# Interleaving runs of 8 words instead of halves 256 words apart in the moving operands of the dense products

## The chip, the core and the metric

The program runs on one core of a Trainium2 chip: TensorE (PE) multiplies, ScalarE (ACT), VectorE (DVE) and GpSimd (POOL) work on vectors, SyncE (SP) issues the transfers. The metric is the device time of one execution in microseconds (us), lower is better. A product on PE has a stationary operand, loaded first, and a moving operand, of which it takes one column after the other from the on-chip memory (SBUF); its sums go to PSUM.

## What is computed

Attention over 4 x 8 heads of 576 positions, a soft mixture of 8 experts, and then a dense part, which the change is about:

```python
def _moe2_ref(x, w_in, w_out):            # x 2304 x 512, w_in 512 x 2048, w_out 2048 x 512
    h = x @ w_in
    g = np.where(h > 0.0, h, np.exp(np.minimum(h, 0.0)) - 1.0)
    return (g @ w_out).astype(np.float32)
```

`w_in` and `w_out` arrive as 64-bit floats and are made 32-bit ones on the chip.

## The kernel before

The mixture's result has rank 32, so its output is never formed. `c4` holds the combining weights of the tokens and `M4` the 32 expert slots times `w_in`, and `h` is the product of the two. Both are kept as a high and a low part, stacked over the 128 partitions. `emit_ct` copies parts of `c4` into `cTf` (the first 2304 words of the tile `pers`): for each of the 4 stacked blocks `a` and each batch `b` of 576 tokens, cut where a group of 512 tokens ends, by ACT, POOL or DVE.

The dense part is a list of units. A unit is a group of 512 tokens (the last group has 256) and one of 16 slices `f` of 128 hidden columns. For each there is one product `hps` (`f_h`, L1276) of 128 x 512, then on ACT and DVE the function (`f_e` L1282, `f_r` L1285, `f_g` L1288) and a high and a low part of the result (L1294, L1298), then for each 128 tokens three products of 128 x 512 into one PSUM tile (`f_o`, L1329 to L1331: high x high, high x low, low x high), in the format fp32r. The very first unit (256 tokens) does it in full 32-bit format with one product, which runs as two passes (L1322). At the end of a run of units a sum is taken out of PSUM (L1364 on ACT, L1366 and L1370 on DVE).

Beside this run the decodes of the weights, per 128 x 512 words: one instruction on ACT that reads every second word (`dec_abs`, L992), and three on DVE (L996, and L1000 and L1006, which read every second word of the 64-bit tile), and for `w_out` a high and a low part (L1225, L1228). `w_in` goes on through `m_nodes` (L1165 to L1192) into `M4`; the products L1183 and L1184 there are the only fp32r ones of 128 x 512 whose moving operand is read word after word.

The order of the dense part is made by a planner (`list_order`): each step is a node with an assumed cost, what it needs and a due time, and the steps are written out engine by engine in the planner's order. The cost that `decode_nodes` gives to `dec_abs` is one of these numbers.

The two helpers `turns` and `pairs` say in which order an operand's columns are walked. In the kernel before, `turns` takes the first word of the first half, the first word of the second half, the second word of the first half and so on, so that consecutive words are 256 words (1 KB) apart in a 512-word slice. What lies in the operand is permuted to fit: the host permutes the columns of `w_out`, and `emit_ct` writes `cTf` in that order. The results come out in natural order, and `pairs` on an output is the same as walking it word after word.

Of the kernel before, what the change touches and what calls it, by code (L numbers as in the profile page):

```python
# [9 lines left out]
F32R = mybir.dt.float32r  # L10
I32 = mybir.dt.int32
BF16 = mybir.dt.bfloat16
AF = mybir.ActivationFunctionType
# [6 lines left out]
def attn_moe_mlp(ctx, tc, q, k, v_l, v_s, phi, w1, w2, w_in, w_out, out):  # L20
    nc = tc.nc
    B, S, D = 4, q.shape[2] // 4, 64
    NT, DM = out.shape
# [44 lines left out]
        39: (-7.7, 3.0), 232: (-14.4, 9.2), 964: (0.0, 14.7),  # L68
    }
    FULL = 1  # L70
    PO, PH = 0.648, 0.216
    FT, FW, M0 = 7.5, 0.9, ((0, 128), (128, 128), (256, 256))

    const = ctx.enter_context(tc.tile_pool(name="const", bufs=1))
# [168 lines left out]
    for x in ORDER:  # L243
        p = {"L": 0, "S": 2}[x]
        p += cnt_p[p] == (6 if p == 0 else 4)
        c = cnt_p[p]
# [10 lines left out]
    with tc.manual_schedule():  # L257
# [18 lines left out]
        for b in range(B):  # L276
            lm = lcur[32 * b:32 * b + 32]
            nc.gpsimd.affine_select(
                out=lm, in_=lm, compare_op=ALU.is_ge, fill=0.0, base=0, pattern=[[-1, 32]], channel_multiplier=1,
# [4 lines left out]
            out=lkeep[:, 0], in0=lkeep[:, 1], scalar1=0.0, scalar2=None, op0=ALU.is_equal  # L284
# [8 lines left out]
        for b in range(B):  # L293
# [3 lines left out]
                out=sm_, in_=sm_, compare_op=ALU.is_ge, fill=0.0, base=0, pattern=[[-1, MR]], channel_multiplier=1,  # L297
# [140 lines left out]
        for n, (p, t, h) in enumerate(units):  # L438
# [4 lines left out]
            else:  # L443
                c = 1152 * t + 576 * h
# [579 lines left out]
        M4 = pers[:, NT:NT + DFF].bitcast(F32R)  # L1024
        e0r = e0.bitcast(F32R)

        groups = [(t, min(512, NT - t)) for t in range(0, NT, 512)]

        def turns(v):
            return v.rearrange("p (a x) -> p x a", a=2)  # L1030

        def pairs(v):
            return v.rearrange("p (x a) -> p x a", a=2)

        def emit_ct(eng, a, b):
            for t0, n in groups:
                u0, u1 = max(t0, S * b), min(t0 + n, S * b + S)
                if u0 >= u1:
                    continue
                o = turns(cTf[32 * a:32 * a + 32, t0:t0 + n])[:, (u0 - t0) // 2:(u1 - t0) // 2]  # L1040
                i = pairs(c4[32 * b:32 * b + 32, a // 2, u0 - S * b:u1 - S * b].bitcast(F32R))
                if eng == "A":
                    nc.scalar.activation(out=o, in_=i, func=AF.Copy)
                else:
                    (nc.vector if eng == "V" else nc.gpsimd).tensor_copy(out=o, in_=i)

        for e in range(NE - 1):
            emit_w2(e)
# [49 lines left out]
        ps_out = ctx.enter_context(tc.tile_pool(name="ps_out", bufs=6, space=PSUM))  # L1098

        NF = DFF // 128  # L1100
        dec_of = {("w", 0, c): dec[:, c] for c in range(4)}
        wo_hi, wo_lo = {}, {}
        wo_hi[0], wo_lo[0] = slot(2, "wh0"), slot(4, "wl0")
# [14 lines left out]
        def node(eng, dur, deps, key, fn, alloc=None, at=0.0):  # L1118
            kd, hold = HOLD.get(len(nodes), (0.0, -9.0))
            nodes.append((eng, dur, list(deps), key + kd, fn, alloc, max(at, hold)))  # L1120
            return len(nodes) - 1
# [16 lines left out]
        def decode_nodes(kind, i, c, key, rel, h0=0):  # L1138
            at = loads.get((1 - kind, i, c), loads.get((1 - kind, i), 0.0))
            deps = [] if at else [dma[1 - kind, i]]  # L1140
            k, z, h = ("ow"[kind], i, c), (512 - h0) / 512, slice(h0, 512)

            def f_abs():
                if not h0:
                    cnt["dec"] += 1
                    dec_of[k] = dec[:, cnt["dec"] % 8]
                dec_abs(w64[1 - kind, i][:, c, h], dec_of[k][:, h])

            def step(f):
                return lambda: f(w64[1 - kind, i][:, c, h], dec_of[k][:, h])  # L1150

            n = node("A", 0.05 + 0.47 * z, deps, key - 3.0, f_abs, None if h0 else ("dec", rel), at)
            n = node("V", 0.065 + 0.27 * z, [n], key - 2.0, step(dec_1))
            n = node("V", 0.07 + 0.53 * z, [n], key - 1.4, step(dec_2))
            n = node("V", 0.07 + 0.53 * z, [n], key - 0.7, step(dec_3))
            d3[1 - kind, i, c, h0] = n
            return n
# [57 lines left out]
        def w_tile(d, s, f):  # L1215
            if f // 8 not in d:
                d[f // 8] = slot(s, f"w{f}")
            return d[f // 8][:, 512 * (f % 8):512 * (f % 8) + 512]
# [49 lines left out]
        def unit_nodes(u):  # L1268
            si, gi, f, f0, f1 = work[u]
            t0, n = groups[gi]  # L1270
            z, T, t = n / 512, due[u], {}
            rel_h, rel_g, rel_hi, rel_lo = [], [], [], []

            def f_h():
                t["ps"] = ps_h.tile([128, 512], F32, tag="h", name="hps")[:, 0:n]
                nc.tensor.matmul(  # L1276
                    pairs(t["ps"]), M4[:, 128 * f:128 * f + 128], turns(cTf[:, t0:t0 + n]), start=True, stop=True
                )

            def f_e():  # L1280
                t["g"] = p2.tile([128, 512], F32, tag="g", name="g", bufs=3)[:, 0:n]
                nc.scalar.activation(out=t["g"], in_=t["ps"], func=AF.Exp)  # L1282

            def f_r():
                nc.scalar.activation(out=t["g"], in_=t["g"], func=AF.Relu, scale=-1.0, bias=1.0)  # L1285

            def f_g():
                nc.vector.scalar_tensor_tensor(  # L1288
                    out=t["g"], in0=t["ps"], scalar=0.0, in1=t["g"], op0=ALU.max, op1=ALU.subtract
                )  # L1290

            def f_hi():
                t["hi"] = ring("hi")[:, 0:n]
                nc.scalar.activation(out=t["hi"], in_=t["g"], func=AF.Copy)  # L1294

            def f_lo():
                t["lo"] = ring("lo")[:, 0:n]
                nc.vector.tensor_tensor(out=t["lo"], in0=t["g"], in1=t["hi"].bitcast(F32), op=ALU.subtract)  # L1298

            def link(k, x):  # L1300
                if k in chain:
                    nodes[x][2].append(chain[k])
                chain[k] = x
                return x

            x = link("h", node("P", PH * z, [m_done[f]], T - 4.1 - SL, f_h, ("h", rel_h)))
            x = link("e", node("A", 0.05 + 0.43 * z, [x], T - 3.7 - SL, f_e, ("g", rel_g)))
            x = node("A", 0.09 + 0.43 * z, [x], T - 3.0 - SL, f_r)
            x = node("V", 0.07 + 0.53 * z, [x], T - 2.3 - SL, f_g)
            rel_h.append(x)  # L1310
            full = u < FULL
            if not full:
                x = link("hi", node("A", 0.09 + 0.43 * z, [x], T - 1.5 - SL, f_hi, ("hi", rel_hi)))
                x = link("lo", node("V", 0.07 + 0.53 * z, [x], T - 0.8 - SL, f_lo, ("lo", rel_lo)))
                rel_g.append(x)
            for s in range(n // 128):
                def f_o(s=s):
                    if f == f0:
                        ops[si, gi, s] = ps_out.tile([128, DM], F32, tag="o", name="ops")
                    o, c = ops[si, gi, s], slice(128 * s, 128 * s + 128)  # L1320
                    if full:
                        nc.tensor.matmul(  # L1322
                            pairs(o), t["g"][:, c], turns(dec_of["o", f // 4, f % 4]), start=(f == f0), stop=False
                        )
                        return
                    hi, lo = turns(w_tile(wo_hi, 0, f).bitcast(F32R)), turns(w_tile(wo_lo, 5, f).bitcast(F32R))
                    for x in halves(u, s):
                        y, q = pairs(o[:, x]), slice(x.start // 2, x.stop // 2)
                        nc.tensor.matmul(y, t["hi"][:, c], hi[:, q], start=(f == f0), stop=False)  # L1329
                        nc.tensor.matmul(y, t["hi"][:, c], lo[:, q], start=False, stop=False)  # L1330
                        nc.tensor.matmul(y, t["lo"][:, c], hi[:, q], start=False, stop=(f == f1 - 1 and x.stop == 512))  # L1331

                rel_o = []
                y = link("o", node("P", 0.9 if full else PO, [x, d3[1, f // 4, f % 4, 0] if full else w_done[f]],
                                   T + PO * s, f_o, ("o", rel_o) if f == f0 else None))
                if full:
                    rel_g.append(y)
                    w_rel[f].append(y)
                else:
                    rel_hi.append(y)  # L1340
                    rel_lo.append(y)
                if f == f0:
                    o_rel.append(rel_o)
                    o_due.append(T + PO * s)
                    part_n[si, gi, s] = len(o_rel) - 1
                if f == f1 - 1:
                    ev_n.append((si, gi, s, f0, f1, y, T + PO * s, halves(u, s)))
# [51 lines left out]
def _lay(np, q, k, v, moe_phi, **rest):  # L1399
# [15 lines left out]
    w1, w2 = ((w.reshape(w.shape[0], -1, 128, w.shape[2]).transpose(0, 2, 1, 3).reshape(w.shape[0], 128, -1))  # L1415
              for w in (rest["moe_w1"], rest["moe_w2"]))
    wo = rest["moe2_w_out"]
    wo = wo.reshape(wo.shape[0], -1, 2).transpose(0, 2, 1).reshape(wo.shape)
    return dict(rest, moe2_w_out=wo, q=lay(q), k=lay(k), v_l=vl, v_s=vs, moe_phi=phi, moe_w1=w1, moe_w2=w2)


# [23 lines left out]
```

## Time and profile before

| | us |
|---|---|
| median of 3 runs (353.8 to 354.85) | 354.21 |
| the profiled execution | 354.27 |
| its span, first to last instruction | 352.6 |
| busy in the span: PE, DVE, ACT, POOL | 332.7, 268.7, 256.3, 63.1 |

The dense part starts at 128 us of the span and ends with it. Before it lie attention (to about 84 us) and the experts, of which the last weights land at 124 us. [...] A product's recorded duration, 379 ns for 128 x 512, overlaps the next one's; the distance between two starts is what a product costs. The same holds for ACT and DVE when they have no gap: there the distance from start to start counts.

### The profile page before, as it was taken

Reading aid. Unit: us, or ns where it says so; the run is one execution under the profiler, and the core shown is the slowest. Engines: PE = TensorE matmul, PEld = TensorE weight load, DVE = VectorE, ACT = ScalarE, POOL = GpSimd, SP = SyncE. Lnnn points to the kernel's source line nnn. Section 1 sums busy time; section 2 is a strip of 40 time slices with the busy share of each in tenths; the row PEclk is TensorE's granted clock in tenths of the full one; section 3 lists DMA queues with packets and bytes.
Section 4 is the critical chain, followed back from the end, with each engine's and each line's share of the span. In section 5 each row is a group of like instructions: output and inputs, shape, how many; then the busy total and the mean of one; then the engine's idle time right before and its main releaser. Section 6 shows DMA issues by size and latency. Waiting matters only on the chain.

```text
span 352.6 us, 7011 instructions
## 1 busy us (share of the span) xinstructions
PE 332.7 (94%) x2679; PEld 251.4 (71%) x2679; DVE 268.7 (76%) x576; ACT 256.3 (73%) x494; POOL 63.1 (18%) x114
## 2 busy tenths in 40 slices
PE   5789889999999999999999999999999999999995
PEld 4678776773233356687887588887878888888884
DVE  6899888744705349999999999999984775576752
ACT  9588999983217359999998786966676666666660
POOL 8888534530209200000000000000000000000000
PEclk9999999999999999999999999999999999999999
DMA  7999999999999999670000606000000011033301
GB/s 270 403 414 414 424 416 422 425 412 421 420 432 416 407 400 374 231 269 0 3 0 0 241 0 237 3 0 0 2 0 2 2 59 59 2 119 119 119 3 60
DMA packets 15329, 70.51 MB, mean 200 GB/s; under 512 B 1600, under 2 KB 2112, under 8 KB 12352
## 3 DMA queue, kind: packets, MB, share of 16 engines
q1 hardware_dynamic: 15296, 70.06, 49.8%
q8 instruction: 21, 0.34, 0.4%
q14 instruction: 12, 0.10, 0.1%
HBM read 65.34 MB, written 4.72 MB: 199 GB/s over the span
## 4 chain that ended last, share of the span: by engine, by line
PE 55%; DVE 17%; ACT 15%; DMA 8%; issue 3%; POOL 2%; DVEq 0%; SPq 0%; POOLq 0%; ACTq 0%
PE ops L1329 13%; PE ops L1331 13%; PE ops L1330 13%; DMA q<-in_moe_w_dram 6%; PE hps L1276 3%; PE s_ps L924 3%; ACT xw L992 2%; ACT bd L658 2%; ACT g L1285 2%; DVE sc L590 2%; ACT g L1282 2%; PE o_ps L671 2%; ACT part L1364 2%; DVE g L1288 2%; DVE xw L1006 2%
## 5 line engine op out<-in xcount | busy, mean ns | idle before, releaser
L1288 DVE SCALAR_TENSOR_TENSOR g<-hps,g 128x512 f32<-128x512 f32 (+1 forms) x80 | 51.1, 639 | 13.1 <-ACT g L1285 12.7
L1282 ACT ACTIVATE g<-hps 128x512 f32<-128x512 f32 (+1 forms) x80 | 45.3, 567 | 8.7 <-PE hps L1276 7.5
L1285 ACT ACTIVATE g<-g 128x512 f32<-128x512 f32 (+1 forms) x80 | 47.9, 599 | 1.3
L1294 ACT ACTIVATE ghi<-g 128x512 fp32r<-128x512 f32 (+1 forms) x40 | 23.8, 595 | 17.6 <-DVE g L1288 15.6
L1294 ACT ACTIVATE rings<-g 128x512 fp32r<-128x512 f32 (+1 forms) x39 | 23.9, 612 | 15.9 <-DVE g L1288 15.1
L1331 PE MATMUL ops<-w,glo 128*128 128x512 f32 (+1 forms) x93 | 35.0, 377 | 0.0
L1276 PE MATMUL hps<-pers 128*128 128x512 f32 (+1 forms) x80 | 30.5, 383 | 1.9 <-DVE g L1288 1.6
L1329 PE MATMUL ops<-wh,rings 128*128 128x512 f32 x80 | 31.1, 389 | 0.8 <-ACT part L1364 0.5
L1329 PE MATMUL ops<-w,ghi 128*128 128x512 f32 (+1 forms) x81 | 30.6, 378 | 0.0
L1330 PE MATMUL ops<-w,ghi 128*128 128x512 f32 (+1 forms) x81 | 30.5, 376 | 0.0
L1330 PE MATMUL ops<-wl,rings 128*128 128x512 f32 x80 | 30.3, 379 | 0.0
L1331 PE MATMUL ops<-wh,glo 128*128 128x512 f32 x80 | 30.3, 379 | 0.0
L658 ACT ACTIVATE bd<-tr 32x288 f32<-32x288 f32 (+1 forms) x60 | 28.7, 479 | 1.3
L1329 PE MATMUL ops<-w,rings 128*128 128x512 f32 x64 | 24.3, 379 | 0.0
L1330 PE MATMUL ops<-w,rings 128*128 128x512 f32 x64 | 24.3, 379 | 0.0
L1331 PE MATMUL ops<-wh,rings 128*128 128x512 f32 x62 | 23.6, 381 | 0.0
L1329 PE MATMUL ops<-wh,ghi 128*128 128x512 f32 x62 | 23.5, 379 | 0.0
L1330 PE MATMUL ops<-wl,ghi 128*128 128x512 f32 x62 | 23.5, 379 | 0.0
L1276 PEld LDWEIGHTS hps<-pers 128*128 128x128 f32 x80 | 15.1, 188 | 9.1 <-DVE g L1288 5.8
L1298 DVE TENSOR_TENSOR glo<-g,ghi 128x512 fp32r<-128x512 f32 (+1 forms) x24 | 15.4, 641 | 6.5 <-ACT ghi L1294 6.4
L1331 PE MATMUL ops<-w,rings 128*128 128x512 f32 x52 | 19.7, 379 | 0.0
L1331 PEld LDWEIGHTS ops<-w,glo 128*128 128x128 f32 x93 | 17.6, 189 | 2.4
(230 smaller groups left out, 793.2 us busy)
## 6 DMA issues: line engine op xcount, KB each, us to landing
v<-in_moe_w_dram SPq DMA_DIRECT2D x3, 2048.0 KB, 12.2
w<-in_moe_w_in_dram SPq DMA_DIRECT2D x3, 2048.0 KB, 7.7
out_dram<-ob SPq DMA_DIRECT2D x17, 256.0 KB, 2.0
w<-in_moe_w_dram SPq DMA_DIRECT2D x2, 2048.0 KB, 11.8
xw<-in_moe_w_dram SPq DMA_DIRECT2D x4, 1024.0 KB, 12.6
xw<-in_moe_w_out_dram SPq DMA_DIRECT2D x2, 2048.0 KB, 7.8
q<-in_q_dram SPq DMA_DIRECT2D x6, 576.0 KB, 7.9
kB<-in_k_dram SPq DMA_DIRECT2D x8, 288.0 KB, 7.4
```

What stands on the lines that cost most here:

```text
L590: nc.vector.copy_predicated(out=sc1[:, 8 * hh:8 * hh + 8], mask=spred[:, y:y + 1].to_broadcast([128, 8, MR]), data=z["sc", hh][:, :, y],)
L658: nc.scalar.activation(out=o, in_=i, func=AF.Copy)
L924: nc.tensor.matmul(hp[32 * g:32 * g + 32, :], siT[:, POS[c], :], w_at(2 * a + g // 2, 0, 2 * c + g % 2), start=(c == CO[0]), stop=(c == CO ...
L1276: nc.tensor.matmul(pairs(t["ps"]), M4[:, 128 * f:128 * f + 128], turns(cTf[:, t0:t0 + n]), start=True, stop=True)
L1282: nc.scalar.activation(out=t["g"], in_=t["ps"], func=AF.Exp)
L1285: nc.scalar.activation(out=t["g"], in_=t["g"], func=AF.Relu, scale=-1.0, bias=1.0)
L1288: nc.vector.scalar_tensor_tensor(out=t["g"], in0=t["ps"], scalar=0.0, in1=t["g"], op0=ALU.max, op1=ALU.subtract)
L1294: nc.scalar.activation(out=t["hi"], in_=t["g"], func=AF.Copy)
L1298: nc.vector.tensor_tensor(out=t["lo"], in0=t["g"], in1=t["hi"].bitcast(F32), op=ALU.subtract)
L1329: nc.tensor.matmul(y, t["hi"][:, c], hi[:, q], start=(f == f0), stop=False)
L1330: nc.tensor.matmul(y, t["hi"][:, c], lo[:, q], start=False, stop=False)
L1331: nc.tensor.matmul(y, t["lo"][:, c], hi[:, q], start=False, stop=(f == f1 - 1 and x.stop == 512))
```

## The change

`turns` and `pairs` get a third level. The operand is taken in blocks of 16 words: the first word of the first 8, the first of the second 8, the second of the first 8, and so on. Consecutive words are now 8 words (32 bytes) apart, and a block is used up before the next one begins. The host's permutation of `w_out` follows. Since 576 is a multiple of 16, `emit_ct` need not cut at groups any more and writes 576 words at once: 16 copies in place of 32. The list `groups` moves down, as `emit_ct` no longer uses it. Apart from that the planner's cost of `dec_abs` becomes 0.57 in place of 0.52 for 512 words, which changes its order.

```diff
-    PO, PH = 0.648, 0.216
+    PO, PH, RUN = 0.648, 0.216, 8
...
         def turns(v):
-            return v.rearrange("p (a x) -> p x a", a=2)
+            return v.rearrange("p (g a x) -> p g x a", a=2, x=RUN)
 
         def pairs(v):
-            return v.rearrange("p (x a) -> p x a", a=2)
+            return v.rearrange("p (g x a) -> p g x a", a=2, x=RUN)
 
         def emit_ct(eng, a, b):
-            for t0, n in groups:
-                u0, u1 = max(t0, S * b), min(t0 + n, S * b + S)
-                if u0 >= u1:
-                    continue
-                o = turns(cTf[32 * a:32 * a + 32, t0:t0 + n])[:, (u0 - t0) // 2:(u1 - t0) // 2]
-                i = pairs(c4[32 * b:32 * b + 32, a // 2, u0 - S * b:u1 - S * b].bitcast(F32R))
...
+            o = turns(cTf[32 * a:32 * a + 32, S * b:S * b + S])
+            i = pairs(c4[32 * b:32 * b + 32, a // 2].bitcast(F32R))
...
-            n = node("A", 0.05 + 0.47 * z, deps, key - 3.0, f_abs, None if h0 else ("dec", rel), at)
+            n = node("A", 0.05 + 0.52 * z, deps, key - 3.0, f_abs, None if h0 else ("dec", rel), at)
...
-                    hi, lo = turns(w_tile(wo_hi, 0, f).bitcast(F32R)), turns(w_tile(wo_lo, 5, f).bitcast(F32R))
+                    hi, lo = w_tile(wo_hi, 0, f).bitcast(F32R), w_tile(wo_lo, 5, f).bitcast(F32R)
                     for x in halves(u, s):
-                        y, q = pairs(o[:, x]), slice(x.start // 2, x.stop // 2)
-                        nc.tensor.matmul(y, t["hi"][:, c], hi[:, q], start=(f == f0), stop=False)
+                        y, wh, wl = pairs(o[:, x]), turns(hi[:, x]), turns(lo[:, x])
+                        nc.tensor.matmul(y, t["hi"][:, c], wh, start=(f == f0), stop=False)
...
-    wo = wo.reshape(wo.shape[0], -1, 2).transpose(0, 2, 1).reshape(wo.shape)
+    wo = wo.reshape(wo.shape[0], -1, 8, 2).transpose(0, 1, 3, 2).reshape(wo.shape)
```

ACT's copies by `emit_ct` (`pers` is the tile with `cTf`, `c` is `c4`), which stand in the experts' stage, before:

```order
L992 ACTIVATE xw<-kA 128x256
L1043 ACTIVATE pers<-c_1492 32x256x2
L1043 ACTIVATE pers<-c_1492 32x32x2
L1043 ACTIVATE pers<-c_1492 32x256x2
L1043 ACTIVATE pers<-c_1492 32x32x2
L1043 ACTIVATE pers<-c_1492 32x224x2
...
L1043 ACTIVATE pers<-c_1492 32x128x2
L1079 ACTIVATE y_1763<-o_ps_99 128x256
```

and after:

```order
L992 ACTIVATE xw<-q_103 128x256
L992 ACTIVATE xw<-kB 128x256
L992 ACTIVATE xw<-kA 128x256
L1037 ACTIVATE pers<-c_1492 32x36x8x2 x6
L1073 ACTIVATE y_1747<-o_ps_99 128x256
```

Twelve copies on ACT become six at the same place; POOL's 16 become eight and DVE's four become two.

PE early in the dense part, where the second slice of `M4` is first worked on (`mps`, a product of the decoded `w_in`), before:

```order
L1331 MATMUL ops<-wh_1808,glo_1814 128x512
L1276 MATMUL hps<-pers 128x512
L1329 MATMUL ops<-wh_1808,rings 128x512
L1330 MATMUL ops<-wl_1809,rings 128x512
L1331 MATMUL ops<-wh_1808,glo_1815 128x512
L1329 MATMUL ops<-wh_1808,rings 128x512
L1330 MATMUL ops<-wl_1809,rings 128x512
L1331 MATMUL ops<-wh_1808,glo_1815 128x512
L1165 MATMUL mps<-xw,soT 32x256 x4
```

and after:

```order
L1326 MATMUL ops<-wh_1792,glo_1798 128x512
L1160 MATMUL mps<-xw,soT 32x256 x4
L1324 MATMUL ops<-wh_1792,rings 128x512
L1325 MATMUL ops<-wl_1793,rings 128x512
L1326 MATMUL ops<-wh_1792,glo_1799 128x512
L1324 MATMUL ops<-wh_1792,rings 128x512
L1325 MATMUL ops<-wl_1793,rings 128x512
L1326 MATMUL ops<-wh_1792,glo_1799 128x512
L1181 MATMUL mps<-mp,e_62 128x256
L1271 MATMUL hps<-pers 128x512
```

The `mps` products move ahead of six products into PSUM, and a `hps` behind them. Such exchanges are all that the order of PE shows; the number of products is the same, but for one filler.

ACT at the first decodes of the dense part (`w_0_0` is the tile with `w_in`), before:

```order
L992 ACTIVATE xw<-w_0_0_1755 128x256
L1294 ACTIVATE rings<-g 128x512
L1225 ACTIVATE wh_1808<-xw 128x512
L1282 ACTIVATE g<-hps 128x512
L1294 ACTIVATE ghi_1811<-g 128x256
L1285 ACTIVATE g<-g 128x512
L992 ACTIVATE xw<-xw 128x512 x2
```

and after:

```order
L1220 ACTIVATE wh_1792<-xw 128x512
L1289 ACTIVATE rings<-g 128x512
L1277 ACTIVATE g<-hps 128x512
L1289 ACTIVATE ghi_1795<-g 128x256
L1280 ACTIVATE g<-g 128x512
L992 ACTIVATE xw<-w_0_0_1739 128x256
L992 ACTIVATE xw<-xw 128x512 x2
```

A decode of 256 words moves behind five steps of the units. SP's order is unchanged.

## Rows read from the trace of the kernel before

**Rows 1.** Stages: window, length, busy us of PE, PEld, DVE, ACT, POOL; clock; DMA.
```profile
100.00:125.00 25.00, 23.93 (x199) 7.60 (x192) 8.43 (x22) 10.10 (x18) 10.96 (x16) 1.00 1.01 415
...
150.00:175.00 25.00, 24.47 (x113) 19.36 (x112) 24.76 (x42) 25.00 (x46) 0.00 (x0) 1.00 0.26 93
175.00:200.00 25.00, 23.93 (x113) 19.29 (x111) 24.82 (x42) 21.50 (x38) 0.00 (x0) 1.00 0.23 85
...
275.00:300.00 25.00, 25.00 (x118) 21.89 (x117) 16.33 (x25) 16.57 (x27) 0.00 (x0) 1.00 0.12 43
```

**Rows 2.** Chain that ended last, 100 to 128 us: start, us, what.
```profile
101.35 22.54 DMA q<-in_moe_w_dram
```

**Rows 3.** PE in order of time, 262 us: start, us, instruction.
```profile
261.95 0.38 PE L1330 MATMUL ops<-w,ghi 128*128 128x512 f32 x1
262.17 0.38 PE L1331 MATMUL ops<-w,glo 128*128 128x512 f32 x1
262.38 0.39 PE L1183 MATMUL mps<-mp,e 128*128 128x512 f32 x1
262.61 0.40 PE L1184 MATMUL mps<-ml,e 128*128 128x512 f32 x1
262.84 0.38 PE L1329 MATMUL ops<-w,ghi 128*128 128x512 f32 x1
```

**Rows 4.** Groups by line and shape, 135 to 353 us: count | busy, mean ns | idle before.
```profile
L1329 PE MATMUL ops<-wh,rings 128*128 128x512 f32 x80 | 31.1, 389 | 0.8 <-ACT part L1364 0.5 <-DVE part L1366 0.3
...
L1276 PE MATMUL hps<-pers 128*128 128x512 f32 x62 | 24.7, 399 | 1.9 <-DVE g L1288 1.6 <-DVE pers L1192 0.4
...
L1329 PE MATMUL ops<-wh,ghi 128*128 128x512 f32 x62 | 23.5, 379 | 0.0
...
L1006 DVE SCALAR_TENSOR_TENSOR xw<-w,xw 128x512 int32<-128x512 int32 x16 | 13.1, 826 | 0.0
...
L1006 DVE SCALAR_TENSOR_TENSOR xw<-xw 128x512 int32<-128x512 int32 x10 | 8.3, 829 | 0.0
```

**Rows 5.** Line 1276 on PE: what its engine sat idle for, us, times.
```profile
  DVE g L1288: 7.4, 15
```

**Rows 6.** Line 1329: duration min/median/max, first and last start; its engine's idle time.
```profile
L1329 PE MATMUL ops<-w,ghi x81: 273/379/483, 214.3 to 348.1; 128*128 128x512 f32 x79, 128*128 128x256 f32 x2
...
  ACT part L1364: 1.6, 3
```

**Rows 7.** DVE in order of time, before the dense stream and inside it.
```profile
131.88 0.69 DVE L1000 SCALAR_TENSOR_TENSOR xw<-xw 128x512 int32<-128x512 int32 x1
132.48 0.28 DVE L996 TENSOR_SCALAR xw<-xw 128x256 int32<-128x256 int32 x1
...
175.74 0.83 DVE L1000 SCALAR_TENSOR_TENSOR xw<-w,xw 128x512 int32<-128x512 int32 x1
176.49 0.68 DVE L1298 TENSOR_TENSOR rings<-g,ghi 128x512 fp32r<-128x512 f32 x1
```

**Rows 8.** ACT in order of time, in the experts' stage and inside the dense stream.
```profile
109.10 0.44 ACT L992 ACTIVATE xw<-kB 128x256 f32<-128x256 f32 x1
109.43 0.44 ACT L992 ACTIVATE xw<-kA 128x256 f32<-128x256 f32 x1
...
177.55 1.04 ACT L992 ACTIVATE xw<-w 128x512 f32<-128x512 f32 x1
178.30 0.81 ACT L1294 ACTIVATE rings<-g 128x512 fp32r<-128x512 f32 x1
```

**Rows 9.** Lines 1043 and 1045: durations, first and last start.
```profile
L1043 ACT ACTIVATE pers<-c x12: 313/718/1166, 109.8 to 116.7; 32x512 fp32r<-32x512 f32 x2, 32x64 fp32r<-32x64 f32 x2, 32x384 fp32r<-32x384 f32 x2, 32x192 fp32r<-32x192 f32 x2
L1045 POOL CAST pers<-c x16: 292/836/1122, 105.3 to 115.8; 32x512 fp32r<-32x512 f32 x2, 32x64 fp32r<-32x64 f32 x2, 32x448 fp32r<-32x448 f32 x2, 32x128 fp32r<-32x128 f32 x2
```

**Rows 10.** PE in order of time at the first unit.
```profile
132.23 2.32 PE L1322 MATMUL ops<-xw,g 128*128 128x512 f32 x4
...
134.61 0.39 PE L1390 MATMUL wps<-ident 128*128 128x256 bf16 x2
```

More of the change, by code (lines that the diff above doesn't have):

```diff
@@ L1025, in attn_moe_mlp @@
         e0r = e0.bitcast(F32R)
-        groups = [(t, min(512, NT - t)) for t in range(0, NT, 512)]
         def turns(v):
-            return v.rearrange("p (a x) -> p x a", a=2)
+            return v.rearrange("p (g a x) -> p g x a", a=2, x=RUN)
         def pairs(v):
-            return v.rearrange("p (x a) -> p x a", a=2)
+            return v.rearrange("p (g x a) -> p g x a", a=2, x=RUN)
         def emit_ct(eng, a, b):
-            for t0, n in groups:
-                u0, u1 = max(t0, S * b), min(t0 + n, S * b + S)
-                if u0 >= u1:
-                    continue
-                o = turns(cTf[32 * a:32 * a + 32, t0:t0 + n])[:, (u0 - t0) // 2:(u1 - t0) // 2]
-                i = pairs(c4[32 * b:32 * b + 32, a // 2, u0 - S * b:u1 - S * b].bitcast(F32R))
[L1042 to L1045, printed above, removed]
+            o = turns(cTf[32 * a:32 * a + 32, S * b:S * b + S])
+            i = pairs(c4[32 * b:32 * b + 32, a // 2].bitcast(F32R))
+            if eng == "A":
+                nc.scalar.activation(out=o, in_=i, func=AF.Copy)
+            else:
+                (nc.vector if eng == "V" else nc.gpsimd).tensor_copy(out=o, in_=i)
         for e in range(NE - 1):
@@ L1100, in attn_moe_mlp @@
         NF = DFF // 128
+        groups = [(t, min(512, NT - t)) for t in range(0, NT, 512)]
         dec_of = {("w", 0, c): dec[:, c] for c in range(4)}
@@ L1325, in f_o @@
                         return
-                    hi, lo = turns(w_tile(wo_hi, 0, f).bitcast(F32R)), turns(w_tile(wo_lo, 5, f).bitcast(F32R))
+                    hi, lo = w_tile(wo_hi, 0, f).bitcast(F32R), w_tile(wo_lo, 5, f).bitcast(F32R)
                     for x in halves(u, s):
-                        y, q = pairs(o[:, x]), slice(x.start // 2, x.stop // 2)
-                        nc.tensor.matmul(y, t["hi"][:, c], hi[:, q], start=(f == f0), stop=False)
-                        nc.tensor.matmul(y, t["hi"][:, c], lo[:, q], start=False, stop=False)
-                        nc.tensor.matmul(y, t["lo"][:, c], hi[:, q], start=False, stop=(f == f1 - 1 and x.stop == 512))
+                        y, wh, wl = pairs(o[:, x]), turns(hi[:, x]), turns(lo[:, x])
+                        nc.tensor.matmul(y, t["hi"][:, c], wh, start=(f == f0), stop=False)
+                        nc.tensor.matmul(y, t["hi"][:, c], wl, start=False, stop=False)
+                        nc.tensor.matmul(y, t["lo"][:, c], wh, start=False, stop=(f == f1 - 1 and x.stop == 512))
                 rel_o = []
```

## Prediction

> **What bounds the kernel now.** I read the stages first, then the chain, then single instructions. From 100 to 125 us the transfers run at 415 GB/s without a pause while ACT works 10.10 of 25 us, DVE 8.43 and POOL 10.96 [rows 1]. The chain says the same: 22.54 us of waiting for the experts' last weights, from 101.35 to 123.89 us [rows 2]. Nothing that ACT, DVE or POOL do in that stretch is on the path as long as it is done by 124 us. From 150 us on DVE is full (24.76 and 24.82 of 25 us), ACT full until 175 us, and PE still runs nearly without a pause; from 275 us PE alone is full [rows 1]. So the dense part has two limits. Before some 262 us, DVE and ACT carry the decodes beside the units, and PE now and then waits for them: 7.4 us in 15 waits of an `hps` for DVE's `g` [rows 5], and 1.6 us for ACT to take a sum out of PSUM [rows 6]. After 262 us only PE's products count, to the last one at 348.1 us [rows 6].
>
> What does a product cost? Inside the stream the starts stand at 261.95, 262.17 and 262.38, so 0.215 us apart [rows 3]. [...] The row beside it is the one that matters most for the change: the two products whose moving operand is read word after word start at 262.38 and 262.61 and the next at 262.84, 0.23 us each [rows 3]. So the order of the words is worth about 15 ns of a product, and the alternating walk is the quicker of the two.
>
> A second row tells what the stream does to others. A decode on DVE that reads every second word took 131.88 to 132.48, 0.60 us, before the stream, and 175.74 to 176.49, 0.75 us, inside it [rows 7]; steps that read word after word do not show that. On ACT a decode of 256 words took 0.33 us at 109 us, so 512 take at most 0.66, and inside the stream 177.55 to 178.30, 0.75 us [rows 8]. PE's stream slows the readers that skip words. Whether its moving or its stationary operand does so is not told by these rows.
>
> **The change part by part.**
>
> *The pitch of the products.* There are four groups of L1329, the largest x80 and the smallest x62, 285 in all; with L1330 and L1331 three times that, 855, and 62 wide `hps` with the narrow ones worth 7 [rows 4]: 924 products of 512 columns. The new walk is still alternating, each word from another run than the one ahead, so by its nearest row, the alternating one, it costs 0.215 us: change 0. The other bound is the word-after-word row, 0.23 us, since a block of 16 words is now used up before the next, as in a straight walk. That bound is +15 ns x 924 = 13.9 us gross. I take 0, as the alternation is what differs between the two rows, and keep both ends. [...]
>
> *The decodes beside the stream.* They read the same words in the same step. Their price can move only if the stream presses less or more on them. Whole relief would be 0.15 us for each of the 52 reads by L1000 and L1006 (26 each, x16 and x10 [rows 4]), 7.8 us of DVE time, and at least 0.09 us for each of ACT's 26. I take 0, as both walks change the run with every word, and keep -7.4 us as an end: more than PE's waits for DVE cannot be won [rows 5]. On the other side, if the reads get slower again by half of what the stream cost them, 0.075 us x 52 = 3.9 us of DVE time, and in a stage where DVE is full all of it can come to the end.
>
> *The copies of `emit_ct`.* ACT's twelve begin at 109.8 and the last begins at 116.7; POOL's sixteen run from 105.3 to 115.8 plus one more [rows 9]. Eight pieces of POOL and six of ACT go away. The weights' landing at 123.89 hides all of it [rows 2], so the gain is 0. If the longer pieces with the new step took twice as long a word, POOL's 11.3 us would become 22.6, to 128 us, about where the dense part starts; a loss there would need more than that. I take 0.
>
> *The full-precision unit.* The four passes of L1322, with one wide `hps` behind them, run from 132.23 to 134.61, so (2.38 - 0.22) / 4 = 0.54 us each [rows 10], and an `hps` behind them stands in line for DVE's `g` anyway. At the stream's two passes in 0.43 us they would give back 4 x 0.11 = 0.4 us; the end cannot see more than that. I take 0.
>
> *The order.* The planner's 0.05 us for each `dec_abs` makes it move decodes behind unit steps on ACT, and on PE an `mps` ahead of six products. The work on each engine is the same, and in the stretch concerned DVE and ACT are full [rows 1], so their sum and not their order sets when `hps` can go on. An exchange moves single waits of about 0.5 us (7.4 us in 15 [rows 5]), some longer, some shorter. I take 0 with two such waits on either side, 1 us.
>
> Sum, against the profiled execution's own 354.27 us (the span of 352.6 and 1.7 around it): 354.27 + 0 = 354.3. The median of the runs is 0.06 us lower, 354.2, and that is the forecast.
>
> [...] Rows 7 and 8 show 0.60 against 0.75 us and at most 0.66 against 0.75 us beside the stream. [...]
>
> **The rivals.**
>
> *Less pressure on the decodes, faster.* For it: the new walk stays inside 64 bytes until they are used up, as a straight walk does, and the readers that suffer are those that skip words. Against it: it still changes the run with every word. Half the relief is 3.7 us: 350.6 us; all of it 346.9.
>
> *The straight walk's pitch, slower.* If what makes 0.215 out of 0.23 is the distance between the runs and not the alternation, 32 bytes are too near. After 262.84 us there are (348.1 - 262.84) / 0.215 = 397 products and no wait to swallow anything: 6.0 us, so 360.2 us. Before that 527 products would add 7.9 us, of which the 7.4 us of waits can swallow nearly all; if they swallow nothing it is 368.1. A pitch halfway gives 357.2. It decides from about 1.1 us on the whole, which is 2.7 ns a product after 262 us.
>
> *More pressure on the decodes, slower.* Words 32 bytes apart may press on the same part of the memory as a reader that goes straight through it. Half as much again gives 3.9 us: 358.2 us. Nothing in the rows speaks for more rather than less.
>
> *It does nothing but reorder.* The operand's new walk has three levels in place of two and the same words; if neither pitch nor pressure changes, the planner's exchange is all, and that is my first case: 353.3 to 355.3 us.
>
> **How the numbers follow.** First case, no change beyond the order: 0.36. Less pressure: 0.32. The straight walk's pitch, in whole or in part: 0.23. More pressure: 0.09. A measurement of this kernel tells about 0.3% from no change, 1.06 us. Of the first case 0.05 lies beyond that on either side. Less pressure is faster but for 0.01 of it; the third case is slower but for 0.02, the fourth but for 0.01. So faster 0.36, same 0.30, slower 0.34. The range: below, the first rival to 5.3 us, 349.0, leaving out 0.07; above, the second to 360.0, leaving out 0.10. The likeliest case alone would have 353.3 to 355.3 us.
>
> **What would show it.** Starts of L1329 to L1331 in the stage after 275 us (lines 1324 to 1326 in the changed kernel): 0.215 us apart for the first case, 0.23 for the second rival. L1000 and L1006 in the stretch where DVE is full: 0.75 us from start to start, 0.60 for the first rival, 0.82 for the third. The copies of `emit_ct` done before 124 us. The waits of `hps` for DVE near 7 us. A transfer or PE's clock that looks otherwise in the dense part would make the whole sum wrong, since nothing in it moves them.

## The result, and the profile after

| | median us | runs from | ratio to before, 95% interval |
|---|---|---|---|
| before | 354.27 | 353.8 to 354.85 | |
| after | 350.08 | 349.81 to 350.35 | 0.9881 [0.9864, 0.9898] |

The change is worth 4.2 us. The profiled execution of after took 350.35 us, its span 348.6. This is the place and almost the size of the first rival, "less pressure on the decodes, faster" (350.6), and not the forecast, "no change beyond the order" (353.3 to 355.3). The experiments show that the 4.2 is a sum of two parts of opposite sign.

The stages of after (window, length, busy us and instructions of PE, PEld, DVE, ACT, POOL, clock, DMA share, GB/s), to be read beside [rows 1]:

```profile
100.00:125.00 25.00, 24.32 (x208) 8.00 (x202) 9.63 (x20) 10.02 (x12) 9.92 (x8) 1.00 1.00 416
...
150.00:175.00 25.00, 25.00 (x119) 20.83 (x119) 24.30 (x44) 24.95 (x48) 0.00 (x0) 1.00 0.22 84
175.00:200.00 25.00, 25.00 (x119) 20.78 (x119) 24.75 (x44) 21.00 (x41) 0.00 (x0) 1.00 0.23 85
...
275.00:300.00 25.00, 25.00 (x118) 21.89 (x117) 14.81 (x22) 16.63 (x28) 0.00 (x0) 1.00 0.11 43
```

The instruction counts tell more than the busy times. From 150 to 200 us PE gets through 119 products in each stretch in place of 113, with DVE nearly as full as before; DVE and ACT get through more instructions in the same full 25 us (44 for 42, 48 for 46). From 275 us, where PE alone is full, it is 118 both times. So the gain arises while the decodes run, and none of it in the products' own pace.

The line numbers of the dense part are 5 lower than before. PE in order of time (start, us, instruction) answers to [rows 3]:

```profile
268.00 0.38 PE L1324 MATMUL ops<-w,rings 128*128 128x512 f32 x1
268.22 0.38 PE L1325 MATMUL ops<-w,rings 128*128 128x512 f32 x1
268.43 0.38 PE L1326 MATMUL ops<-w,rings 128*128 128x512 f32 x1
```

Still 0.215 us; the median of all distances after 265 us is 216.0 ns in both kernels. The decodes are what has changed. Groups by line and shape (count | busy, mean ns | idle before) in the dense part of after, beside [rows 4], and two places in order of time, beside [rows 7, 8]:

```profile
L1006 DVE SCALAR_TENSOR_TENSOR xw<-w,xw 128x512 int32<-128x512 int32 x16 | 10.8, 682 | 0.0
...
L1006 DVE SCALAR_TENSOR_TENSOR xw<-xw 128x512 int32<-128x512 int32 x10 | 6.7, 682 | 0.0
```

```profile
175.33 0.68 DVE L1006 SCALAR_TENSOR_TENSOR xw<-w,xw 128x512 int32<-128x512 int32 x1
175.94 0.68 DVE L1293 TENSOR_TENSOR rings<-g,ghi 128x512 fp32r<-128x512 f32 x1
```

```profile
179.65 0.69 ACT L992 ACTIVATE xw<-xw 128x512 f32<-128x512 f32 x1
180.22 0.64 ACT L1280 ACTIVATE g<-g 128x512 f32<-128x512 f32 x1
```

L1006 fell from 826 and 829 ns recorded to 682; from start to start it is 0.61 us on DVE, and L992 on ACT is 0.57, where [rows 7, 8] had 0.75 for L1000 and for L992. That is the price [rows 7] showed outside the stream, 0.60: the whole of the relief, not half. As medians over all such steps in the stream: L992 764 ns before and 568 after, L1000 743 and 602, L1006 738 and 601.

What PE waits for, as line 1271's idle time (us, times), beside [rows 5]; and the copies of `emit_ct` (duration min/median/max, first to last start), beside [rows 9]:

```profile
  DVE pers L1187: 1.9, 3
  PE ops L1326: 1.2, 1
  DVE g L1283: 1.1, 3
```

```profile
L1037 ACT ACTIVATE pers<-c x6: 1229/1247/1264, 111.2 to 117.5; 32x576 fp32r<-32x576 f32 x6
...
L1039 POOL CAST pers<-c x8: 1207/1234/1325, 106.7 to 115.7; 32x576 fp32r<-32x576 f32 x8
...
L1039 DVE CAST pers<-c x2: 670/676/683, 119.3 to 120.0; 32x576 fp32r<-32x576 f32 x2
```

The last copy ends at 120.7 us; the chain's wait for the experts' weights (start, us), beside [rows 2], runs to 124.72:

```profile
102.77 21.95 DMA q<-in_moe_w_dram
```

The waits for DVE's `g` fell from 7.4 us in 15 to 1.1 in 3, and the wait for `M4` (`pers`, L1187; 0.4 us before [rows 4]) grew; the section on the order returns to it. These rows of a line take the idle time of its matmuls and of its weight loads together: of the 7.4 us, 1.6 in 4 waits stand before matmuls and 5.8 in 11 before weight loads. Counted by PE's own starts (what the distance to the next start has over 216 ns, from 137 us on), PE lost 9.5 us in 46 places before and 4.6 in 23 after. The last product began at 348.32 us before and at 344.40 after, 3.9 us earlier.

### The profile page after: what moved, and what is told of

It is laid out like the page before. It is cut to its first block, busy times and chain, and to the rows that moved or that the text cites. A ratio compares the mean times of both kernels' runs of the same rounds, so it can differ in the third digit from the quotient of the medians.

```text
span 348.6 us, 6993 instructions
## 1 busy us (share of the span) xinstructions
PE 328.6 (94%) x2678; PEld 251.9 (72%) x2678; DVE 263.9 (76%) x574; ACT 251.4 (72%) x488; POOL 62.1 (18%) x106
## 4 chain that ended last, share of the span: by engine, by line
PE 64%; DVE 13%; ACT 9%; DMA 9%; POOL 2%; issue 2%; DVEq 0%; SPq 0%; POOLq 0%
PE ops L1324 16%; PE ops L1326 15%; PE ops L1325 15%; DMA q<-in_moe_w_dram 6%; PE hps L1271 4%; PE s_ps L924 3%; DMA w<-in_moe_w_in_dram 2%; PE o_ps L671 2%; ACT bd L658 2%; DVE sc L590 2%; DVE g L1283 1%; PE xtps L787 1%; DVE sm L614 1%; DVE xw L1000 1%; DVE ss L605 1%
## 5 line engine op out<-in xcount | busy, mean ns | idle before, releaser
L1277 ACT ACTIVATE g<-hps 128x512 f32<-128x512 f32 (+1 forms) x80 | 44.0, 550 | 9.8 <-PE hps L1271 8.8
L1280 ACT ACTIVATE g<-g 128x512 f32<-128x512 f32 (+1 forms) x80 | 46.8, 585 | 1.2
L1289 ACT ACTIVATE ghi<-g 128x512 fp32r<-128x512 f32 (+1 forms) x40 | 23.2, 581 | 17.1 <-DVE g L1283 15.1
L1326 PE MATMUL ops<-w,glo 128*128 128x512 f32 (+1 forms) x93 | 35.0, 377 | 0.0
L1289 ACT ACTIVATE rings<-g 128x512 fp32r<-128x512 f32 (+1 forms) x39 | 23.3, 598 | 13.5 <-DVE g L1283 12.7
L1324 PE MATMUL ops<-wh,rings 128*128 128x512 f32 x80 | 30.7, 383 | 0.0
L1271 PE MATMUL hps<-pers 128*128 128x512 f32 (+1 forms) x80 | 29.5, 374 | 1.2 <-DVE pers L1187 1.2
L1324 PE MATMUL ops<-w,ghi 128*128 128x512 f32 (+1 forms) x81 | 30.5, 376 | 0.0
L1326 PE MATMUL ops<-wh,glo 128*128 128x512 f32 x80 | 30.3, 379 | 0.0
L1324 PE MATMUL ops<-w,rings 128*128 128x512 f32 x64 | 24.3, 379 | 0.0
L1326 PE MATMUL ops<-wh,rings 128*128 128x512 f32 x62 | 23.6, 381 | 0.4 <-DVE rings L1293 0.4
L1324 PE MATMUL ops<-wh,ghi 128*128 128x512 f32 x62 | 23.6, 381 | 0.0
L671 PE MATMUL o_ps<-bd,v 128*64 128x128 f32 x288 | 19.4, 288 | 1.0 <-ACT bd L658 0.6
L1326 PE MATMUL ops<-w,rings 128*128 128x512 f32 x52 | 19.7, 379 | 0.0
L1326 PEld LDWEIGHTS ops<-w,glo 128*128 128x128 f32 x93 | 17.6, 189 | 2.4
```

Source lines behind the costliest of these rows:

```text
L671: nc.tensor.matmul(o[64 * e:64 * e + 64, j, :], v_t[p][:, max(i - 1 + k, 0), e, :], pt[:, 4 * j + 2 * e + k], start=(k == 0), stop=(k == 1),)
L1271: nc.tensor.matmul(pairs(t["ps"]), M4[:, 128 * f:128 * f + 128], turns(cTf[:, t0:t0 + n]), start=True, stop=True)
L1324: nc.tensor.matmul(y, t["hi"][:, c], wh, start=(f == f0), stop=False)
L1326: nc.tensor.matmul(y, t["lo"][:, c], wh, start=False, stop=(f == f1 - 1 and x.stop == 512))
```

## The experiments

Each part of the change was taken alone first; then the distance between the two runs was varied with all else as in after; last, the disputed cost was measured by itself.

### The two parts apart: `cost_back` and `cost_only`

`cost_back` is after with the planner's old cost; `cost_only` is before with the new one.

```diff
 # cost_back, against after
-            n = node("A", 0.05 + 0.52 * z, deps, key - 3.0, f_abs, None if h0 else ("dec", rel), at)
+            n = node("A", 0.05 + 0.47 * z, deps, key - 3.0, f_abs, None if h0 else ("dec", rel), at)
 # cost_only, against before
-            n = node("A", 0.05 + 0.47 * z, deps, key - 3.0, f_abs, None if h0 else ("dec", rel), at)
+            n = node("A", 0.05 + 0.52 * z, deps, key - 3.0, f_abs, None if h0 else ("dec", rel), at)
```

> The changed kernel with the planner's old cost of the decode (0.52 us) and so the old order. Pressure theory (the runs' distance alone frees the readers that skip words): 350 us within 1, decodes on DVE at 0.60 us from start to start and on ACT at 0.57. Order theory (the planner's exchange is the gain): 353.5 to 354.5 us.

> The kernel before with the planner's new cost of the decode alone. Pressure theory: 353.3 to 355.3 us, decodes at 0.75 us on DVE and 0.76 on ACT as before. Order theory: 350 us.

Measured: `cost_back` 347.84 us, ratio to before 0.9821 [0.9793, 0.9849]; `cost_only` 356.08, 1.0051 [1.0035, 1.0067]. So the walk alone is worth 6.4 us with the old order (354.27 to 347.84) and 6.0 with the new one (356.08 to 350.08), and the new order costs 1.8 us with the old walk and 2.2 with the new. That the order does nothing is refuted, and so is that it brings the gain. `cost_back` beats both kernels. The pressure theory had the order at nothing, so both times lie outside what it expected (349 to 351 and 353.3 to 355.3 us), by 1.2 and 0.8 us.

Where does the new order lose? ACT around 200 us, first after, then `cost_back`, then `cost_only` (start, us, instruction, in brackets the idle time before it and what ended it):

```profile
197.39 0.60 ACT L1167 ACTIVATE mp<-mps 128x512 fp32r<-128x512 f32 x1
199.38 0.68 ACT L992 ACTIVATE xw<-w 128x512 f32<-128x512 f32 x1 [1.40 <-DMA w<-in_moe_w_in_dram]
199.96 0.62 ACT L1289 ACTIVATE rings<-g 128x512 fp32r<-128x512 f32 x1
```

```profile
196.05 0.60 ACT L1167 ACTIVATE mp<-mps 128x512 fp32r<-128x512 f32 x1 [0.30 <-PE mps L1160]
196.54 0.68 ACT L992 ACTIVATE xw<-w 128x512 f32<-128x512 f32 x1
197.10 0.63 ACT L1289 ACTIVATE rings<-g 128x512 fp32r<-128x512 f32 x1
```

```profile
202.88 0.80 ACT L992 ACTIVATE xw<-w 128x512 f32<-128x512 f32 x1 [1.56 <-DMA w<-in_moe_w_in_dram]
...
222.98 0.74 ACT L992 ACTIVATE xw<-xw 128x512 f32<-128x512 f32 x1 [2.12 <-DMA xw<-in_moe_w_out_dram]
```

With the new cost ACT stands before a decode whose words have not landed, and the units' step behind it waits too. What follows from it in after, on DVE and then on PE:

```profile
199.08 0.68 DVE L1006 SCALAR_TENSOR_TENSOR xw<-xw 128x512 int32<-128x512 int32 x1
200.61 0.69 DVE L1293 TENSOR_TENSOR glo<-g,rings 128x512 fp32r<-128x512 f32 x1 [0.85 <-ACT rings L1289]
```

```profile
202.43 0.38 PE L1326 MATMUL ops<-wh,glo 128*128 128x512 f32 x1
203.67 0.45 PE L1271 MATMUL hps<-pers 128*128 128x512 f32 x1 [0.86 <-DVE pers L1187]
```

and in `cost_only`, DVE and then PE:

```profile
204.22 0.69 DVE L1298 TENSOR_TENSOR glo<-g,rings 128x512 fp32r<-128x512 f32 x1 [0.77 <-ACT rings L1294]
...
207.44 0.46 PE L1276 MATMUL hps<-pers 128*128 128x512 f32 x1 [1.03 <-DVE pers L1192]
```

DVE, the full engine, idles 0.85 us for `rings` (L1289), the step behind the decode. Behind it come the sum, `g` and the slice of `M4` (L1187), and PE's `hps` starts 1.24 us after the product ahead of it, 1.0 us more than a product costs; in `cost_only` it starts 1.41 us after, 1.2 us more. The load is late because its issue waits on SP for the last decode that reads the buffer (L1006; in after its last two steps begin at 189.40 us and last 1.28). It went out at these times, in after and in `cost_back` (SP's queue in order of time):

```profile
190.75 0.37 SPq L981 DMA_DIRECT2D w<-in_moe_w_in_dram  x1
```

```profile
188.26 0.37 SPq L981 DMA_DIRECT2D w<-in_moe_w_in_dram  x1
```

The two waits of ACT for a load (1.3 to 1.9 us for `w_in`, 1.9 to 2.2 for `w_out`) stand in all eight kernels of this study that have the new cost and PE's 0.216 us, without the added work of the probe below (in `run1` and `run2`, at 0.227 us, they are 0.6 and 1.3 to 1.4), and neither of them in before or `cost_back`. Inside the dense part (first fp32r product to last) the profiled executions last 213.27 us before, 215.50 `cost_only`, 208.67 after, 207.17 `cost_back`: 2.2 and 1.5 us for the order. Of these, 1.2 and 1.0 are the gap of PE shown above; where the rest arises is not shown. Behind the wait for `w_out` in after, PE has no gap of more than 0.31 us. The other 1.0 us between the profiled executions of after and `cost_back` stands ahead of the dense part, where the experts' weights landed at 124.72 and 123.52 us. The new cost is not what delays them: in `run4`, `w16` and `w32` below, which have it too, they landed at 123.5 to 123.7 us, and the dense part took 208.6 to 209.2. Issuing the load earlier was not tried.

### Which operand presses: `run1`

After with runs of one word, that is word after word, in `turns`, `pairs` and the host's permutation.

```diff
-    PO, PH, RUN = 0.648, 0.216, 8
+    PO, PH, RUN = 0.648, 0.216, 1
...
-    wo = wo.reshape(wo.shape[0], -1, 8, 2).transpose(0, 1, 3, 2).reshape(wo.shape)
+    wo = wo.reshape(wo.shape[0], -1, 1, 2).transpose(0, 1, 3, 2).reshape(wo.shape)
```

> The changed kernel with runs of 1 word, which is reading word after word. If the alternation makes the pitch, 0.23 us a product and 356 to 358 us (6.0 us for the 397 products after the decodes, nothing to some 3 more before them, less nothing else), while the decodes stay at 0.60 and 0.57 us, since the stationary operand's loads are the same and would then be shown not to press. If the stationary operand presses on them, they are at 0.75 us here too. If alternating is not what makes the pitch, 0.215 us and 350 us.

Measured: 358.8 us, 1.0125 [1.0092, 1.0158]. PE in order of time:

```profile
300.33 0.39 PE L1271 MATMUL hps<-pers 128*128 128x512 f32 x1
300.55 0.39 PE L1324 MATMUL ops<-w,ghi 128*128 128x512 f32 x1
300.78 0.39 PE L1325 MATMUL ops<-w,ghi 128*128 128x512 f32 x1
301.01 0.39 PE L1326 MATMUL ops<-w,rings 128*128 128x512 f32 x1
```

The product costs 0.227 us (median 227 ns after 265 us), 11 ns more than in after; 924 products x 11 ns are 10.2 us, less 1.9 us of PE's gaps (4.6 in after, 2.8 here, each over its own distance), 8.3 us, against 8.7 measured to after. That is 0.8 us above the range expected, which let at most 3 us be paid before the decodes were done. The decodes cost 563, 601 and 601 ns, as in after: they are just as free beside a straight walk, with the same stationary loads. So it was the moving operand's far alternation that slowed them to the 764, 743 and 738 ns of before.

### The products of `w_out` back to 1 KB: `w256`

After, but the products of L1324 to L1326 and of the first unit walk `w_out` as before, and `cTf` keeps the new layout with its 16 copies.

```diff
+        def turns_w(v):
+            return v.rearrange("p (g a x) -> p g x a", a=2, x=RW)
...
-                        y, wh, wl = pairs(o[:, x]), turns(hi[:, x]), turns(lo[:, x])
+                        y, q = o[:, x], slice(x.start // 2, x.stop // 2)
+                        wh, wl = turns_w(hi)[:, 0, q], turns_w(lo)[:, 0, q]
...
-    wo = wo.reshape(wo.shape[0], -1, 8, 2).transpose(0, 1, 3, 2).reshape(wo.shape)
+    wo = wo.reshape(wo.shape[0], -1, 256, 2).transpose(0, 1, 3, 2).reshape(wo.shape)
```

> The changed kernel, but the decoded w_out is walked as before, with runs 256 words apart; cTf keeps runs of 8, so the copies are the new ones. Pressure theory: the 855 products with w_out press as before, decodes on DVE at 0.73 to 0.75 us, 353.5 to 354.5 us. If the copies or the products of hps bring the gain: 350 us, decodes at 0.60.

Measured: 355.69 us, 1.0036 [1.002, 1.0052], which is `cost_only`'s time within 0.4 us, and above the 353.5 to 354.5 expected, which had the order at nothing. The decodes are back at 746, 747 and 748 ns. The new copies and `hps` alone bring nothing.

### How near is near: `w16`, `w32`, `w64`, `w128`, `run2`, `run4`

The first four set RW of the helper above to 16, 32, 64 and 128 words, so that the words of the `w_out` walk alternate 64, 128, 256 and 512 bytes apart; the `y` of the products is then `o[:, x]` and the operand `turns_w(hi[:, x])`. `run2` and `run4` set RUN of after to 2 and 4 everywhere: 8 and 16 bytes.

```diff
-    PO, PH, RUN = 0.648, 0.216, 8
+    PO, PH, RUN, RW = 0.648, 0.216, 8, 16
...
-                        y, wh, wl = pairs(o[:, x]), turns(hi[:, x]), turns(lo[:, x])
+                        y, wh, wl = o[:, x], turns_w(hi[:, x]), turns_w(lo[:, x])
```

> As w256, with w_out in runs of 16 words, 64 bytes apart. If a block of 64 bytes is what frees the readers, the pressure is back: decodes on DVE at 0.75 us. If it is the nearness in some wider piece of memory, 0.60 and 350 us. Pitch 0.215 us either way.

> Runs of 32 words, 128 bytes apart: between 0.60 us a decode (350 us) and 0.75 us (355.7 us); the first of w16, w32, w64, w128 that shows 0.75 gives the distance at which the pressure begins, if there is one such distance.

> Runs of 64 words, 256 bytes apart: as for w32. A theory of growing distance expects a decode here no quicker than in w32.

> Runs of 128 words, 512 bytes apart: if only runs a whole 1 KB apart press, 0.60 us a decode and 350 us; if the pressure grows with the distance, close to 0.75 us and 355.7 us.

> Runs of 2 words, 8 bytes apart: the walk 0, 2, 1, 3 stays inside 16 bytes. If alternating as such makes the pitch, 0.216 us a product and 350 us; if the second run has to lie outside 16 bytes, 0.227 us as with word after word, and 358.8 us. Decodes at 0.60 us.

> Runs of 4 words, 16 bytes apart: every word is from the other of two neighbouring pieces of 16 bytes. If alternating between two such pieces makes the pitch, 0.216 us and 350 us; else 0.227 us and 358.8 us. Decodes at 0.60 us.

All have the new cost of the planner, and `cost_only` stands in the table as the walk of before. Distances from start to start in ns, medians inside the stream (which steps are counted moves those of the decodes by up to 10 ns):

| bytes apart | kernel | us | ratio, interval | a product | L992, L1000, L1006 |
|---|---|---|---|---|---|
| word after word | run1 | 358.8 | 1.0125 [1.0092, 1.0158] | 227 | 563, 601, 601 |
| 8 | run2 | 358.54 | 1.0114 [1.0071, 1.0158] | 227 | 564, 602, 601 |
| 16 | run4 | 349.41 | 0.9856 [0.9814, 0.9899] | 216 | 564, 602, 602 |
| 32 | after | 350.08 | 0.9881 [0.9864, 0.9898] | 216 | 568, 602, 601 |
| 64 | w16 | 350.06 | 0.9878 [0.9838, 0.9918] | 216 | 568, 602, 602 |
| 128 | w32 | 349.75 | 0.9869 [0.984, 0.9898] | 216 | 574, 602, 602 |
| 256 | w64 | 355.61 | 1.003 [1.0014, 1.0046] | 216 | 760, 749, 747 |
| 512 | w128 | 355.81 | 1.0033 [1.0017, 1.0049] | 216 | 755, 745, 742 |
| 1024 | cost_only | 356.08 | 1.0051 [1.0035, 1.0067] | 216 | 765, 745, 744 |

Two steps, and nothing in between. The pitch drops from 227 to 216 ns between 8 and 16 bytes: the alternation counts only from 16 bytes on. The decodes jump between 128 and 256 bytes, all at once (L992 574 to 760 ns, L1000 602 to 749, L1006 602 to 747), and then no longer grow with the distance. The two groups of L1006 in `w32` and then in `w64`:

```profile
L1006 DVE SCALAR_TENSOR_TENSOR xw<-w,xw 128x512 int32<-128x512 int32 x16 | 10.8, 686 | 0.0
...
L1006 DVE SCALAR_TENSOR_TENSOR xw<-xw 128x512 int32<-128x512 int32 x10 | 6.7, 682 | 0.0
```

```profile
L1006 DVE SCALAR_TENSOR_TENSOR xw<-w,xw 128x512 int32<-128x512 int32 x16 | 12.8, 810 | 0.0
...
L1006 DVE SCALAR_TENSOR_TENSOR xw<-xw 128x512 int32<-128x512 int32 x10 | 7.5, 770 | 0.0
```

Between 16 and 128 bytes the four kernels cannot be told apart by their intervals.

The 32-bit products of the first unit, which walk `w_out` in the same order, go the other way. Its four passes in `run1` and then in after:

```profile
132.74 1.88 PE L1317 MATMUL ops<-xw,g 128*128 128x512 f32 x4
```

```profile
133.04 2.30 PE L1317 MATMUL ops<-xw,g 128*128 128x512 f32 x4
```

From start to start a pass costs 0.43 us in `run1` and `run2` and 0.53 to 0.55 us in every kernel with 16 bytes or more. There are only four of them, so the time does not show it.

### Which readers are pressed: `probe_before` and `probe_after`

Before and after, each with 24 added steps in the last stage, where PE streams and the decodes are done: pairs of copies of 512 words out of `M4`, on ACT and on DVE, taking every word, every second and every fourth. Their results are not used.

```diff
+        def probe(eng, k, n):
...
+                i = pers[:, NT:NT + n * k].rearrange("p (x k) -> p x k", k=k)[:, :, 0]
+                for _ in range(2):
+                    if eng == "A":
+                        nc.scalar.activation(out=o, in_=i, func=AF.Copy)
+                    else:
+                        nc.vector.tensor_scalar(out=o, in0=i, scalar1=2.0, scalar2=None, op0=ALU.mult)
```

> The kernel before with added copies of 512 words out of M4 in the last stage, where only the units run: pairs on ACT and on DVE with every word, every second and every fourth word read; their results are not used. Pressure theory: every word 0.52 us on ACT and 0.34 on DVE as elsewhere; every second word about 0.75 us on ACT and slower than every word on DVE; every fourth at least as slow. If only the decodes' own tiles or the 64-bit data were the cause, no difference by the step.

> The changed kernel with the same added copies. Pressure theory: every second word at 0.57 us on ACT and as every word on DVE; every fourth word not slower than in the kernel before.

The whole kernels took 361.31 and 350.85 us in one execution each; what counts is the pairs. ACT's in `probe_before` and in `probe_after`, steps 1, 2, 4 and (the second kernel's rows go by time) 4, 1, 2 (start, us of both copies):

```profile
288.82 1.28 ACT L1358 ACTIVATE probe<-pers 128x512 f32<-128x512 f32 x2
...
293.36 1.80 ACT L1358 ACTIVATE probe<-pers 128x512 f32<-128x512 f32 x2
...
297.25 3.17 ACT L1358 ACTIVATE probe<-pers 128x512 f32<-128x512 f32 x2
```

```profile
289.11 2.26 ACT L1353 ACTIVATE probe<-pers 128x512 f32<-128x512 f32 x2
...
293.46 1.27 ACT L1353 ACTIVATE probe<-pers 128x512 f32<-128x512 f32 x2
...
296.68 1.37 ACT L1353 ACTIVATE probe<-pers 128x512 f32<-128x512 f32 x2
```

A reader that takes every word does not notice the far alternation: 1.28 and 1.27. One that takes every second word pays 1.80 in place of 1.37, every fourth 3.17 in place of 2.26. On DVE the first copy of a pair took 0.404 to 0.422 us in `probe_before` and 0.416 to 0.417 in `probe_after` with step 1, 0.479 to 0.525 and 0.418 to 0.427 with step 2, 0.833 to 0.902 and 0.632 to 0.640 with step 4. So the pressure falls on ACT and DVE alike, on readers that skip words, and it is a matter of the read and not of the decode's arithmetic. In absolute size the copies were slower than expected in both kernels (with step 1, 0.65 us from start to start in place of 0.52 on ACT and about 0.45 in place of 0.34 on DVE; in `probe_after`, 0.69 in place of 0.57 with step 2 on ACT); the reading rests on the comparison. Why the step lies between 128 and 256 bytes, the runs do not tell.

## Where the prediction was wrong, and where it was right

**The forecast** was the case with no change beyond the order, 354.2 us. It did not happen, and 350.08 is 4.1 us off. The time fell inside the range because the range reached to the first rival, whose place and mechanism were right. It gave 350.6 for half the relief; what happened is the whole relief, less what the order took back. That the two come out within 0.6 us is luck.

**The step that failed: "The decodes beside the stream. ... I take 0, as both walks change the run with every word."** Not whether the run changes decides, but how far apart the runs are: 602 ns for L1000 at 128 bytes, 749 at 256. The term's end was -7.4 us; the walk alone gave -6.4 and -6.0. The reasoning for that end held: PE's gaps by its own starts fell from 9.5 us to 3.5 in `cost_back`, 6.0 us. The relief itself was larger, 52 reads on DVE by about 0.14 us, 7.2 us, and 26 on ACT by about 0.2, 5.1 us. Only the part for which PE had been waiting came to the end. The prediction held both facts, that the pressure exists [rows 7, 8] and that the operand causing it was untold, and chose 0 for want of a row on distance. That steps which read word after word are not slowed was said there without a row; the probes show it (1.28 and 1.27 us for ACT's two copies with step 1). No row of before had one; a run of `w_out` at another distance was the only way to know.

**The second step that failed: the order, "0 with two such waits on either side, 1 us".** It measured +1.8 and +2.2. "Their sum and not their order sets when `hps` can go on" left out that an order can make the full engine idle: the later load let ACT stand 1.4 us before a decode, and DVE 0.85 us behind ACT. The prediction saw that SP's order was unchanged and did not ask for SP's times, which follow the decode that frees the buffer. That the new cost is nearer the truth (0.57 us assumed, 0.568 measured in after) did not make the order better.

**The pitch: right, and its rival partly too.** Change 0, as taken: 216.0 ns in both. The bound from the word-after-word row, 0.23 us [rows 3], was real: 0.227 word after word or with 8 bytes. That `run1` at 358.8 is near the 360.2 of that rival is in part chance: all 924 products paid, 11 ns and not 15, and the decodes' relief, which that sum did not have, took some of it back. The reason given, "the alternation is what differs", was half of it: 8 bytes alternate too.

**More pressure: did not happen** at any distance; the decodes never got slower than before by more than 10 ns.

**The copies of `emit_ct`: right.** They end before 121 us, the weights land at 124.72 us, and `w256`, which keeps them, gains nothing. They do not take twice as long a word: 1.23 us for 576 on POOL, where before took at most 1.12 for 512.

**The full-precision unit: right.** Its passes cost 0.535 us each after 0.540 before; the 0.4 us did not come. The 0.43 us taken for its end is a real price: `run1` and `run2` have it, at 8 bytes or less.

**That PE's stream slows the readers that skip words: right.** POOL has no instruction in before from 128 us to the end of the dense part, and the decodes and the probes show ACT and DVE taking from 0.05 us (DVE, every second word) to 0.45 us (ACT, every fourth) longer for 512 words according to PE's walk.

## What to carry to other kernels

When PE's moving operand in fp32r is read in turns from two runs, the distance is a size to choose: here 16 to 128 bytes gave the quick product (216 ns in place of 227) and left the decodes on ACT and DVE alone (564 to 574 and 601 to 602 ns), and 256 bytes or more slowed them (742 to 765 ns); at 1 KB every added copy that skips words was slowed too (ACT's pairs 1.80 us in place of 1.37 and 3.17 in place of 2.26). For the 32-bit products the straight walk was the quicker, 0.43 us a pass in place of 0.53 to 0.55. Look for it where a step costs more beside the stream than the same step outside it. And run a changed planner's number apart from the change it came with: here it took back a third of the gain, and more than half of what it took inside the dense part was PE's wait behind a load issued too late for the decode that stood first in line.

## What the runs showed of the hardware that was not expected

The step between 128 and 256 bytes was not expected to be one: the decodes' price is 0.60 us on one side and 0.75 on the other, with nothing between, and flat from there to 1 KB.

Nor was it expected that 16 bytes are what makes an fp32r product quick: 216 ns with 16 bytes to 1 KB, 227 with 8 bytes or word after word. The 32-bit products of the first unit show the opposite order: 0.43 us a pass with 8 bytes or word after word, 0.53 to 0.55 from 16 bytes on.
